# Softmax order in batch 0, and q loaded ahead of v with k projected alone in batch 1: Linformer attention and a maxout MoE layer in one kernel

## Chip, cores and metric

The kernel runs on one core of one Trainium2 chip. The metric is the device time of one execution in microseconds (us); times given for a kernel are medians over executions, and the profile is of one execution.

## The reference, cut to what matters

Eight batches, eight heads, sequence 1024, head dimension 64. Keys and values are first projected along the sequence to 64 rows, so the softmax runs over 64 columns.

```python
k_proj = np.einsum('ks,bhsd->bhkd', E, k)
v_proj = np.einsum('ks,bhsd->bhkd', F, v)
scores = (q @ k_proj.T) / sqrt(64)          # per batch and head
scores = scores - max(scores); attn = exp(scores); attn = attn / sum(attn)
x = (attn @ v_proj), as (8192 tokens, 512)
out = maximum(x @ w1, x @ w2) @ w_out       # w1, w2: 512x1024, w_out: 1024x512
```

All inputs and the output are float32; the kernel works in float16 with float32 sums.

## The kernel before, in words

**Engines.** TensorE does matmuls and transposes into PSUM. VectorE and ScalarE take results out of PSUM. GpSimd (POOL) issues the loads, which change float32 to float16 on their way; SyncE (SP) issues stores and DMA transposes. Each engine runs its instructions in the order in which the program gives them; the order is written out by hand.

**PSUM.** Four single banks (`mm_bank`, handed out in turn from the list `turn`, or by number) and two pairs of banks (`att_banks`, used alternately). A bank or pair is written again only after its last reader.

**A batch's attention.** Heads are worked in groups of four (g = 0, 1) and the tokens in halves (j = 0, 1), so there are four blocks (g, j). The steps, by the names used in the lists of the code: `kv` projects k and v (`step_kv` for a part of the heads in batch 0, `step_kv_sets` for all of them later; k goes to `kp_sb`, v to `vp_sb`), `kpt` transposes the projected k into `kpt`, `qt` transposes q into `qt_sb` on TensorE (batches 0 and 1). For a block: `tp` (`step_top`) computes scores and VectorE takes the row maxima (L340, two reductions); `tt` (`step_topt`) transposes the maxima and ScalarE copies them (L358); `sc` (`step_sc`) computes the scores less their maxima (L372) and ScalarE takes the exponential (L415, 1.02 us); `dn` (`step_dn`) sums the exponentials by a matmul with ones, and ScalarE takes the logarithm (L423); `in` (`step_inv`) takes exp(-log), the inverse (L427); `at` (`step_at`, `AT` with a PSUM pair) multiplies by the values (L387), and VectorE multiplies by the inverse into `xt_sb` (L442).

**The MoE layer.** max(a, b) = b + relu(a - b), so `wd` = w1 - w2 is made on VectorE (`step_wd`), `gt` = relu(x wd) is the up product (L522 in batch 0; `u0`, `u1` are the two halves of the tokens, eight column blocks each), and the output is gt w_out + x (w2 w_out), where w2 w_out is multiplied out once into `m_sb` (`step_w2t` transposes w2 on TensorE with a copy by ScalarE, L554 and L560; `m_steps`, L631). Later batches form up and down products by Strassen's scheme, with sums of blocks on VectorE (`sums_x`, `sums_g`, L703, and `step_t`, L594) and the partial products kept by ScalarE (L717) or added by VectorE (L865).

**Order around the change.** Batch 0's attention is a straight list of calls. After it comes the list `slots`: up products of batch 0, then the pieces of the down product of its first half, keys ("P", 0, p, i), into which batch 1's attention is put: after piece n = 1, 2, ... come the steps named in the n-th string of a list. A piece of unit 0 is six matmuls; p1, p2, ... end with a copy by ScalarE or an addition by VectorE. A step that returns a function leaves its last part (the reductions of `tp`, the copy of `tt`, the copies of v) to be issued after the next slot's own work.

**Loads.** The GpSimd queue is served in order: batch 0's k, q, v, then the weights, then k, v, q of batch 1 and k of batch 2 (`loads`). q of batch 1 comes in two halves by chunk. The tiles are four buffers (`kvq`); v and q of batch 2 are issued after batch 1's projection, because they take the buffers of batch 1's k and of another tile that is then free. q of batch 2 is transposed by DMA (L310).

Three of the calls in batch 0 that the text refers to:

```python
step_kv(t, 0, 4, "v")        # L981, values of heads 0 to 3
step_kv(t, 4, 8, "v", True)  # L1000, values of heads 4 to 7, into a PSUM pair
step_w2t(0, True)            # L1006
```

Of the kernel before, what the change touches and what calls it, by code (L numbers as in the profile page):

```python
# [9 lines left out]
FP16 = mybir.dt.float16  # L10
LN_EXP_SET = 6
ACTF = mybir.ActivationFunctionType
# [4 lines left out]
def kernel(  # L17
# [12 lines left out]
    nc = tc.nc  # L30
# [28 lines left out]
    def mm_bank(dtype=FP32, n=None):  # L59
        if n is None:  # L60
            n = turn.pop(0)
            turn.append(n)
        return ps.tile([128, 512 if dtype == FP32 else 1024], dtype, tag=f"mm{n}", name="mm_ps")

    def att_banks(dtype=FP32):
        return ps.tile(
            [128, 2, 512 if dtype == FP32 else 1024], dtype, tag="att", bufs=2, name="att_ps"
        )
# [116 lines left out]
        t["qt"] = qtp.tile([128, H, HALF], FP16, tag="qt", name="qt_sb")  # L185


    def step_kv(t, h0, h1, which, att=False):
        kv_ps = att_banks()[:, 0, :] if att else mm_bank()
        n = (h1 - h0) * D  # L190
        both = which == "v"
        i = "kv".index(which)
        for c in range(NC):
            for r in range(2) if both else (0,):
                nc.tensor.matmul(
                    out=kv_ps[r * KP : (r + 1) * KP, 0:n],
                    lhsT=eft[i][:, c, :],
                    rhs=t[which][:, h0:h1, c, :],
                    start=(c == 0), stop=(c == NC - 1),
                )  # L200
        if both:
            nc.vector.tensor_copy(
                out=t["vp"][:, h0:h1],
                in_=kv_ps[:, 0:n].rearrange("p (h d z) -> p h z d", d=D // 2, z=2),
            )
        else:
            t["kp"] = soft.tile([KP, 4, 2, D], FP16, tag="soft", name="kp_sb")
            for r, copy in enumerate((nc.vector.tensor_copy, nc.vector.tensor_copy if h0 else nc.scalar.copy)):
                copy(out=t["kp"][:, :, r, :], in_=kv_ps[0:KP, 0:n].rearrange("p (h d) -> p h d", d=D))
# [1 line left out]

    ORDER = (0, 2, 1, 3)

    def step_kv_sets(t, bank=None, copy=nc.scalar.copy):
        late = bank is None
        if late:
            bank = att_banks()[:, 0, :]
        t["sets"] = True
        kp = t["kp"] = proj.tile([128, H // 2 + 1, D], FP16, tag="kp", name="kp_sb")
        n = H // 2 * D  # L220
        for i, w in enumerate("kv"):
            for c in range(NC):
                for s in range(2):
                    nc.tensor.matmul(  # L224
                        out=bank[s * KP : (s + 1) * KP, i * n : (i + 1) * n],
                        lhsT=eft[i][:, c, :],
                        rhs=t[w][:, s * H // 2 : (s + 1) * H // 2, c, :],
                        start=(c == 0 and i == 0), stop=(c == NC - 1), skip_group_check=True,
                    )
        k_ps = bank[:, 0:n].rearrange("p (h d) -> p h d", d=D)  # L230
        copy(out=kp[:, 0 : H // 2, :], in_=k_ps)
        copy(out=kp[:, H // 2, :], in_=k_ps[:, 0, :])

        def finish_v():
            vp, m = t["vp"], H // 2
            nc.vector.tensor_copy(
                out=vp[:, 0:m], in_=bank[:, n : 2 * n].rearrange("p (h d z) -> p h z d", d=D // 2, z=2)
            )
            for a, b in (0, KP), (KP, 0):
                nc.vector.tensor_copy(out=vp[a : a + KP, m:H], in_=vp[b : b + KP, 0:m])  # L240

        if late:
            return finish_v
        finish_v()

    def step_kpt_sets(t):
        kpt_ps = att_banks(FP16)[:, 0, :]
        for i, a in enumerate(ORDER):
            nc.tensor.transpose(  # L249
                out=kpt_ps[:, i * 2 * KP : (i + 1) * 2 * KP],  # L250
                in_=t["kp"][:, a : a + 2, :].rearrange("p h d -> p (h d)"), identity=ident16,
            )
        def finish():
            src = kpt_ps[:, 0 : H * KP].rearrange("q (y x s k) -> q x y s k", y=2, x=2, s=2)
            dst = t["kpt"].rearrange("q (s x y) r k -> q r x y s k", s=2, x=2)
            lo, hi = slice(0, D), slice(D, 128)
            nc.scalar.copy(out=dst[lo, 0], in_=src[lo])
            nc.scalar.copy(out=dst[hi, 1, :, 1], in_=src[hi, :, 0])
            for x in range(2):
                nc.scalar.copy(out=dst[hi, 1, 1 - x, 0], in_=src[hi, x, 1])  # L260

        return finish

    def kpt_of(t, head, o):
        return t["kpt"][o * D : (o + 1) * D, head, o, :]
# [82 lines left out]
    def step_topt(t, g, j):  # L348
        x = t.pop(("top", g, j))
        ps_t = mm_bank(FP16) if t is tiles[0] else att_banks(FP16)[:, 0, :]  # L350
        for i in range(2):
            nc.tensor.transpose(  # L352
                out=ps_t[:, i * 128 : (i + 1) * 128], in_=x[:, i, :], identity=ident16
            )
        t["topt", g, j] = y = proj.tile([128, W], FP16, tag="topt", bufs=4, name="topt_sb")

        def finish():
            nc.scalar.copy(out=y, in_=ps_t[:, 0:W])  # L358

        return finish  # L360
# [47 lines left out]
        return t["xt"][:, 2 * g : 2 * g + 2, :, j * W : (j + 1) * W]  # L408


    def step_sc(t, g, j):
        sc_ps = att_banks()
        t["ps", g, j] = sc_ps
        score(t, g, j, [sc_ps[:, e, :] for e in range(2)])
        nc.scalar.activation(out=t["ex", g, j], in_=sc_ps, func=ACTF.Exp, scale=scale)  # L415

    def step_dn(t, g, j):
        dn_ps = t.pop(("ps", g, j))[:, :, 0:W]
# [6 lines left out]
    def step_inv(t, g, j):  # L425
        ld = t["ld", g, j]
        nc.scalar.activation(out=ld, in_=ld, func=ACTF.Exp, scale=-1.0)  # L427
# [109 lines left out]
    def step_wd(f0, r0=0, r1=NDC, n=256):  # L537
        nc.vector.tensor_tensor(
            out=wd_sb[:, r0:r1, f0 : f0 + n], in0=w1_sb[:, r0:r1, f0 : f0 + n],
            in1=w2_sb[:, r0:r1, f0 : f0 + n], op=ALU.subtract,  # L540
        )
# [433 lines left out]
    step_sc(t, 0, 1)  # L975
    step_dn(t, 0, 0)
    tops = [step_top(t, 1, j) for j in range(2)]
    tops.pop(0)()
    step_topt(t, 1, 0)()
    step_dn(t, 0, 1)  # L980
    step_kv(t, 0, 4, "v")  # L981
    tops.pop(0)()
    step_sc(t, 1, 0)
    for f0 in (0, 128):
        step_wd(f0, 0, 2, 128)
    step_topt(t, 1, 1)()
    step_inv(t, 0, 0)
    first_banks = turn[0:2], turn[2:4]
    step_at(t, 0, 0)
    step_sc(t, 1, 1)  # L990
    step_inv(t, 0, 1)
    step_dn(t, 1, 0)
    step_at(t, 0, 1)
    step_dn(t, 1, 1)
    step_inv(t, 1, 0)
    step_inv(t, 1, 1)
    u0, u1 = [*up_slots(t, 0)], [*up_slots(t, 1)]
    for x in u0[0:2]:
        x(r1=2)
    step_kv(t, 4, 8, "v", True)  # L1000
    for x in u1[0:2]:
        x(r1=2)
    step_wd(0, 2, 4)
    step_at(t, 1, 0, True)
    step_at(t, 1, 1, True)
    step_w2t(0, True)  # L1006


    load_all(tiles[1], 1, "k", k)
# [5 lines left out]
    def loads(b, *names):  # L1015
# [14 lines left out]
                load_all(tiles[b_], b_, n, {"k": k, "v": v, "q": q}[n])  # L1030

    slots = [
        (0, lambda: u0[0](r0=2)), (1, lambda: u0[1](r0=2)), (None, lambda: loads(1, "v", "q", "k")),
        (None, lambda: step_w2t(256, True)),
        (2, lambda: u1[0](r0=2)), (3, lambda: u1[1](r0=2)),
        (None, wd[1]), (4, u0[2]), (5, u0[3]),
        (None, wd[2]), (6, u1[2]), (7, u1[3]), (None, wt[2]), (None, wt[3]), (8, u0[4]), (9, u0[5]), (None, wd[3]),
        (10, u1[4]), (11, u1[5]), (12, u0[6]), (13, u0[7]),
# [45 lines left out]
    at_slot((0, 22), new_attn, t)  # L1084
    at_slot((0, 22), lambda: turn.__setitem__(slice(None), [2, 3]))
    for n, x in enumerate((
        "", "qt00 qt10", "kv", "qt01", "kpt qt11", "tp00", "tp10", "tt00", "tt10 tp01", "tp11", "tt01",
        "tt11", "sc00", "sc10", "dn00 in00", "dn10 in10", "at00", "AT10", "sc01",
    )):
        key = ("P", n // 15, (n - 1) // 2 % 7, (n - 1) % 2) if n else (0, 22)  # L1090
        for name in x.split():
            if name[0] == "k":
                if name == "kpt":
                    at_slot(key, step_kpt_sets, t)
                else:
                    at_slot(key, step_kv_sets, t, None, nc.vector.tensor_copy)
                    at_slot(key, loads, 2, "v", "q")
            else:
                g, j = int(name[2]), int(name[3])
                s_ = {"qt": step_qt, "sc": step_sc,  # L1100
                      "tp": step_top, "tt": step_topt, "dn": step_dn, "in": step_inv, "at": step_at, "AT": step_at}[name[:2]]
                args = (4 * g, 4, 2 * j, 2 * j + 2) if name[:2] == "qt" else (g, j)
                if name[:2] == "qt":
                    s_ = lambda *a: step_qt(*a, copy=nc.scalar.copy)
                at_slot(key, s_, t, *args, *([True] if name[:2] == "AT" else []))
        if n in (1, 4):
            at_slot(key, step_t, 1, (0, 1) if n == 1 else (2, 3))
        if 14 <= n < 18:
            at_slot(key, step_tw, n - 14)
        if 6 <= n < 10:  # L1110
            at_slot(key, sums_x, U[0, 1], ((2, 0, 1, 3)[n - 6],))


    t = tiles[2]
# [107 lines left out]
```

## Time and profile before

| | us |
|---|---|
| median of 3 runs (356.95 to 357.12) | 356.96 |
| the profiled execution | 357.18 |
| its span | 355.4 |
| TensorE busy | 342.1 (96%) |
| VectorE busy | 274.9 (77%) |
| ScalarE busy | 227.6 (64%) |
| batch 0's attention, TensorE | to about 32 |
| batch 1's attention, TensorE | about 51 to 75 |
| granted TensorE clock | 0.999 |

The page gives each engine's busy time, the chain of work that ended last, and the costliest groups of instructions with the idle time before them and what ended it. The timeline gives instructions in order of time, with the idle time of the engine before each and its releaser. A load's landing is its issue plus the time that the DMA view gives for it.

### The profile page before, as it was taken

To read this page: it belongs to the slowest core of one execution; us is meant where nothing else is said; L and a number is where in the kernel's file an instruction comes from. 1 tells how busy PE (TensorE), PEld (TensorE's weight loads), DVE (VectorE), ACT (ScalarE), POOL (GpSimd) and SP (SyncE) were. 2 spreads that over 40 slices of the span, in tenths; PEclk is the share of its full clock that TensorE was granted. 3 is DMA by queue.
4 is the path that set the end of the run, shared out by engine and by line. 5 is a ranking of instruction groups with operands and counts; after the bars stand their busy time and mean duration, and the time that the engine had idled before them with its cause. 6 is when DMAs were issued, how large, how long until landed. Compare 5 with 4: busy or idle time off the path is not lost.

```text
span 355.4 us, 11049 instructions
## 1 busy us (share of the span) xinstructions
PE 342.1 (96%) x4801; PEld 283.3 (80%) x4801; DVE 274.9 (77%) x511; ACT 227.6 (64%) x435; POOL 39.0 (11%) x58
## 2 busy tenths in 40 slices
PE   7878998999999999999999999999999999999996
PEld 3644587667888888888888888888888888888885
DVE  4765875877796969696978969696969869696873
ACT  2376755477776676767675867667674767676542
POOL 8375002020000110003000200003000000000000
PEclk9999999999999999999999999999999999999999
DMA  8999999999201999588993999499976511031223
GB/s 190 206 197 203 208 201 191 196 153 207 45 30 49 191 166 218 155 164 163 203 263 106 181 185 226 121 174 174 211 159 102 138 55 67 16 105 35 86 90 118
DMA packets 73713, 52.87 MB, mean 149 GB/s; under 512 B 26817, under 2 KB 73281, under 8 KB 73665
## 3 DMA queue, kind: packets, MB, share of 16 engines
q0 software_dynamic: 30688, 28.05, 50.0%
q1 hardware_dynamic: 42688, 23.93, 27.6%
q8 instruction: 37, 0.61, 0.7%
q10 hardware_dynamic: 288, 0.20, 0.2%
q14 instruction: 12, 0.09, 0.1%
HBM read 57.15 MB, written 16.78 MB: 208 GB/s over the span
## 4 chain that ended last, share of the span: by engine, by line
PE 75%; DVE 0%; ACT 0%; issue 0%; DVEq 0%
PE mm_ps L835 38%; PE mm_ps L743 24%; PE mm_ps L372 4%; PE att_ps L331 3%; PE mm_ps L224 3%; PE att_ps L387 3%; PE att_ps L352 1%; PE att_ps L249 0%; DVE o_sb L933 0%; PE mm_ps L927 0%; ACT p_sb L717 0%; ACT kpt L260 0%; DVEq L933 0%
## 5 line engine op out<-in xcount | busy, mean ns | idle before, releaser
L717 ACT COPY p_sb<-mm_ps 128x512 f32<-128x512 f32 x179 | 101.3, 592 | 57.7 <-PE mm_ps L743 32.4
L835 PEld LDWEIGHTS <-big 128*128 128x128 f16 x768 | 72.3, 98 | 10.6 <-issue 3.2
L835 PE MATMUL mm_ps<-T_sb,big 128*128 128x256 f16 x576 | 77.2, 273 | 0.0
L758 DVE TENSOR_TENSOR gt_sb<-mm_ps,p_sb 128x512 f16<-128x512 f32 x56 | 38.4, 686 | 42.7 <-PE mm_ps L743 41.3
L743 PE MATMUL mm_ps<-big,big 128*128 128x256 f16 x336 | 50.4, 273 | 0.7 <-ACT p_sb L717 0.7
L743 PEld LDWEIGHTS <-big 128*128 128x128 f16 x448 | 43.8, 98 | 6.0 <-issue 0.9
L835 PE MATMUL mm_ps<-wo_sb,gt_sb 128*128 128x256 f16 x256 | 43.0, 273 | 0.0
L468 ACT ACTIVATE ex_sb<-mm_ps 128x512 f16<-128x512 f32 x50 | 27.1, 594 | 20.1 <-PE att_ps L387 11.4
L835 PEld LDWEIGHTS <-gt_sb 128*128 128x128 f16 x376 | 34.3, 98 | 7.0 <-issue 3.6
L340 DVE TENSOR_REDUCE top<-att_ps 128x8 f16<-128x512 f32 x56 | 36.1, 689 | 3.6 <-PE att_ps L331 3.6
L743 PEld LDWEIGHTS <-wd_sb 128*128 128x128 f16 x336 | 32.9, 98 | 3.8
L743 PE MATMUL mm_ps<-xt_sb,wd_sb 128*128 128x256 f16 x224 | 32.8, 273 | 0.0
L497 DVE TENSOR_TENSOR xt_sb<-att_ps,ld_sb 128x1024 f16<-128x1024 f32 x26 | 31.6, 1214 | 0.0
L865 DVE TENSOR_TENSOR o_sb<-mm_ps,p_sb 128x512 f32<-128x512 f32 x32 | 21.8, 681 | 4.4 <-PE mm_ps L835 2.4
L835 PE MATMUL mm_ps<-m_sb,xt_sb 128*128 128x256 f16 x128 | 24.5, 273 | 0.0
L290 POOL COPY junk<-qt_sb 1x1 f16<-1x1 f16 x6 | 1.8, 298 | 202.1 <-DMA qt_sb<-q_sb 202.1
L761 DVE TENSOR_SCALAR gt_sb<-gt_sb 128x512 f16<-128x512 f16 (+1 forms) x60 | 21.8, 363 | 2.1
L703 DVE TENSOR_TENSOR big<-gt_sb 128x1024 f16<-128x1024 f16 x32 | 21.8, 681 | 0.0
L835 PE MATMUL mm_ps<-wo_sb,big 128*128 128x256 f16 x128 | 21.5, 273 | 0.0
L835 PE MATMUL mm_ps<-T_sb,gt_sb 128*128 128x256 f16 x120 | 20.3, 273 | 0.0
L835 PEld LDWEIGHTS <-xt_sb 128*128 128x128 f16 x188 | 18.2, 98 | 2.4 <-issue 0.2
L804 ACT ACTIVATE gt_sb<-mm_ps 128x512 f16<-128x512 f32 x28 | 17.0, 606 | 4.6 <-PE mm_ps L743 4.6
(138 smaller groups left out, 554.0 us busy)
## 6 DMA issues: line engine op xcount, KB each, us to landing
out_dram<-o_sb SPq DMA_DIRECT2D x62, 256.0 KB, 2.6
k_sb<-in_k_dram POOLq DMA_DIRECT2D x7, 1024.0 KB, 9.3
v_sb<-in_v_dram POOLq DMA_DIRECT2D x7, 1024.0 KB, 14.1
q_sb<-in_q_dram POOLq DMA_DIRECT2D x5, 1024.0 KB, 21.4
q_sb<-in_q_dram POOLq DMA_DIRECT2D x6, 512.0 KB, 11.8
big<-in_moe_w_dram POOLq DMA_DIRECT2D x12, 128.0 KB, 6.3
v_sb<-in_v_dram POOLq DMA_DIRECT2D x4, 256.0 KB, 13.8
wo_sb<-in_moe_w_out_dram POOLq DMA_DIRECT2D x1, 1024.0 KB, 10.4
```

The costliest lines, as they stand in the source:

```text
L340: nc.vector.tensor_reduce(out=top[k][:, i, :].rearrange("p (o h) -> p h o", o=2)[:, 0:4, :], in_=banks[i].rearrange("p (h o k) -> p h o k" ...
L372: nc.tensor.matmul(out=banks[e][pos : pos + Z, h * W : (h + 1) * W], lhsT=pick[rows, 2 * h + e, :] if shift else kpt_of(t, head, o)[:, s * ...
L468: nc.scalar.activation(out=t["ex", g, j][:, e, :], in_=banks[e], func=ACTF.Exp, scale=scale)
L497: nc.vector.tensor_tensor(out=x_out(t, g, j).rearrange("q z o n -> q o z n"), in0=at_ps.rearrange("q o (z n) -> q o z n", z=2), in1=ld[:, ...
L703: nc.vector.tensor_tensor(out=S(i), in0=S(0) if x is None else x, in1=y(), op=op)
L717: copy(out=x, in_=bank)
L743: nc.tensor.matmul(out=bank[:, m * W : (m + 1) * W], lhsT=w_[:, n_, (2 * d + m) * 128 : (2 * d + m + 1) * 128], rhs=a[:, n_, :], start=(n ...
L758: nc.vector.tensor_tensor(out=c_blk(j, c), in0=two(x), in1=two(y), op=ALU.add)
L761: nc.vector.tensor_scalar_max(ap, ap, 0.0)
L804: nc.scalar.activation(out=out, in_=in_, func=ACTF.Relu)
L835: nc.tensor.matmul(out=bank[i][:, 0:CH] if two_banks else bank[:, i * CH : (i + 1) * CH], lhsT=a(c)[:, i * 128 : (i + 1) * 128], rhs=w_(c) ...
L865: nc.vector.tensor_tensor(out=o_sb, in0=two(x), in1=two(y), op=ALU.add)
```

## The change

In batch 0 the four reductions of heads 4 to 7 are issued in a row, ahead of the copy of the first projected values; the second projection of v (heads 4 to 7) comes between the scores of block (1, 1) and the sums of block (1, 0) and uses a single bank, the one that `turn` names next, instead of a pair; the last exponential is issued after the logarithm of block (1, 0); values, inverses and the first half of the up products are interleaved anew; `step_w2t(0)` moves behind the second half of `u0`, `step_w2t(256)` behind that of `u1`.

In batch 1 q is loaded ahead of v; `step_kv_sets` can project k or v alone: k at n = 1 (`kk`), its transposes and all four copies at n = 3 (`kpt`), v at n = 8 (`kv`); the q tiles of j = 1 are copied by VectorE instead of ScalarE; the steps from `qt` on are one slot later up to `sc10` and `dn`, and `at00` keeps its slot; the sums of x move from n = 6 to 9 to n = 2 to 5; v of batch 2 is issued after `kk`, q of batch 2 at n = 5.

```diff
-    def step_kv(t, h0, h1, which, att=False):
-        kv_ps = att_banks()[:, 0, :] if att else mm_bank()
+    def step_kv(t, h0, h1, which, bank=None):
+        kv_ps = mm_bank(n=bank)
...
-    def step_kv_sets(t, bank=None, copy=nc.scalar.copy):
+    def step_kv_sets(t, bank=None, copy=nc.scalar.copy, which="kv"):
...
         for i, w in enumerate("kv"):
+            if w not in which:
+                continue
...
+        if "k" in which:
+            kp = t["kp"] = proj.tile([128, H // 2 + 1, D], FP16, tag="kp", name="kp_sb")
+            k_ps = bank[:, 0:n].rearrange("p (h d) -> p h d", d=D)
+            copy(out=kp[:, 0 : H // 2, :], in_=k_ps)
+            copy(out=kp[:, H // 2, :], in_=k_ps[:, 0, :])
+            if which == "k":
+                return
...
-    def step_sc(t, g, j):
+    def step_sc(t, g, j, later=False):
...
-        nc.scalar.activation(out=t["ex", g, j], in_=sc_ps, func=ACTF.Exp, scale=scale)
+
+        def finish():
+            nc.scalar.activation(out=t["ex", g, j], in_=sc_ps, func=ACTF.Exp, scale=scale)
+
+        if later:
+            return finish
+        finish()
...
     step_dn(t, 0, 0)
     tops = [step_top(t, 1, j) for j in range(2)]
-    tops.pop(0)()
+    for finish in tops:
+        finish()
     step_topt(t, 1, 0)()
     step_dn(t, 0, 1)
     step_kv(t, 0, 4, "v")
-    tops.pop(0)()
+    step_inv(t, 0, 0)
+    step_topt(t, 1, 1)()
     step_sc(t, 1, 0)
+    step_at(t, 0, 0)
     for f0 in (0, 128):
         step_wd(f0, 0, 2, 128)
-    step_topt(t, 1, 1)()
-    step_inv(t, 0, 0)
-    first_banks = turn[0:2], turn[2:4]
-    step_at(t, 0, 0)
-    step_sc(t, 1, 1)
+    finish = step_sc(t, 1, 1, True)
+    step_kv(t, 4, 8, "v", turn[0])
     step_inv(t, 0, 1)
     step_dn(t, 1, 0)
+    finish()
     step_at(t, 0, 1)
-    step_dn(t, 1, 1)
-    step_inv(t, 1, 0)
-    step_inv(t, 1, 1)
+    first_banks = turn[0:2], turn[2:4]
     u0, u1 = [*up_slots(t, 0)], [*up_slots(t, 1)]
     for x in u0[0:2]:
         x(r1=2)
-    step_kv(t, 4, 8, "v", True)
+    step_wd(0, 2, 4)
+    step_inv(t, 1, 0)
+    step_at(t, 1, 0, True)
+    step_dn(t, 1, 1)
+    step_inv(t, 1, 1)
     for x in u1[0:2]:
         x(r1=2)
-    step_wd(0, 2, 4)
-    step_at(t, 1, 0, True)
     step_at(t, 1, 1, True)
-    step_w2t(0, True)
...
-        (0, lambda: u0[0](r0=2)), (1, lambda: u0[1](r0=2)), (None, lambda: loads(1, "v", "q", "k")),
+        (0, lambda: u0[0](r0=2)), (1, lambda: u0[1](r0=2)), (None, lambda: loads(1, "q", "v", "k")),
+        (None, lambda: step_w2t(0, True)),
+        (2, lambda: u1[0](r0=2)), (3, lambda: u1[1](r0=2)),
         (None, lambda: step_w2t(256, True)),
-        (2, lambda: u1[0](r0=2)), (3, lambda: u1[1](r0=2)),
...
-        "", "qt00 qt10", "kv", "qt01", "kpt qt11", "tp00", "tp10", "tt00", "tt10 tp01", "tp11", "tt01",
-        "tt11", "sc00", "sc10", "dn00 in00", "dn10 in10", "at00", "AT10", "sc01",
+        "", "kk", "qt00 qt10", "kpt", "qt01", "qt11 tp00", "tp10", "tt00", "kv tt10", "tp01", "tp11", "tt01",
+        "tt11", "sc00", "sc10", "dn00 in00", "dn10 in10 at00", "AT10", "sc01",
...
-                    at_slot(key, step_kv_sets, t, None, nc.vector.tensor_copy)
-                    at_slot(key, loads, 2, "v", "q")
+            if name == "kk":
+                at_slot(key, step_kv_sets, t, None, nc.vector.tensor_copy, "k")
+                at_slot(key, loads, 2, "v")
+            elif name == "kv":
+                at_slot(key, step_kv_sets, t, None, nc.vector.tensor_copy, "v")
+            elif name == "kpt":
+                at_slot(key, step_kpt_sets, t, 0)
...
-                if name[:2] == "qt":
+                if name[:2] == "qt" and j == 0:
                     s_ = lambda *a: step_qt(*a, copy=nc.scalar.copy)
...
-        if 6 <= n < 10:
-            at_slot(key, sums_x, U[0, 1], ((2, 0, 1, 3)[n - 6],))
+        if n == 5:
+            at_slot(key, loads, 2, "q")
+        if 2 <= n < 6:
+            at_slot(key, sums_x, U[0, 1], ((2, 0, 1, 3)[n - 2],))
```

`step_kpt_sets` gets an argument `parts`: with 2 its last two copies are left for a further slot, with 0 all four are issued at once.

More of the change, by code (lines that the diff above doesn't have):

```diff
@@ L218, in step_kv_sets @@
         t["sets"] = True
-        kp = t["kp"] = proj.tile([128, H // 2 + 1, D], FP16, tag="kp", name="kp_sb")
         n = H // 2 * D
         for i, w in enumerate("kv"):
+            if w not in which:
+                continue
             for c in range(NC):
@@ L227, in step_kv_sets @@
                         rhs=t[w][:, s * H // 2 : (s + 1) * H // 2, c, :],
-                        start=(c == 0 and i == 0), stop=(c == NC - 1), skip_group_check=True,
+                        start=(c == 0 and w == which[0]), stop=(c == NC - 1), skip_group_check=True,
                     )
-        k_ps = bank[:, 0:n].rearrange("p (h d) -> p h d", d=D)
-        copy(out=kp[:, 0 : H // 2, :], in_=k_ps)
-        copy(out=kp[:, H // 2, :], in_=k_ps[:, 0, :])
+        if "k" in which:
[5 more added lines that the diff above has]
+                return
         def finish_v():
@@ L244, in step_kv_sets, with step_kpt_sets @@
         finish_v()
-    def step_kpt_sets(t):
+    def step_kpt_sets(t, parts=2):
         kpt_ps = att_banks(FP16)[:, 0, :]
@@ L258, in finish, with rest @@
             nc.scalar.copy(out=dst[hi, 1, :, 1], in_=src[hi, :, 0])
-            for x in range(2):
-                nc.scalar.copy(out=dst[hi, 1, 1 - x, 0], in_=src[hi, x, 1])
-        return finish
+            def rest():
+                for x in range(2):
+                    nc.scalar.copy(out=dst[hi, 1, 1 - x, 0], in_=src[hi, x, 1])
+            if parts == 2:
+                return rest
+            rest()
+        if parts == 0:
+            finish()
+        else:
+            return finish
     def kpt_of(t, head, o):
@@ L414, in step_sc @@
         score(t, g, j, [sc_ps[:, e, :] for e in range(2)])
-        nc.scalar.activation(out=t["ex", g, j], in_=sc_ps, func=ACTF.Exp, scale=scale)
+        def finish():
+            nc.scalar.activation(out=t["ex", g, j], in_=sc_ps, func=ACTF.Exp, scale=scale)
+        if later:
+            return finish
+        finish()
     def step_dn(t, g, j):
@@ L981 @@
     step_kv(t, 0, 4, "v")
-    tops.pop(0)()
+    step_inv(t, 0, 0)
+    step_topt(t, 1, 1)()
     step_sc(t, 1, 0)
+    step_at(t, 0, 0)
     for f0 in (0, 128):
         step_wd(f0, 0, 2, 128)
-    step_topt(t, 1, 1)()
-    step_inv(t, 0, 0)
-    first_banks = turn[0:2], turn[2:4]
-    step_at(t, 0, 0)
-    step_sc(t, 1, 1)
+    finish = step_sc(t, 1, 1, True)
+    step_kv(t, 4, 8, "v", turn[0])
     step_inv(t, 0, 1)
     step_dn(t, 1, 0)
+    finish()
     step_at(t, 0, 1)
-    step_dn(t, 1, 1)
-    step_inv(t, 1, 0)
-    step_inv(t, 1, 1)
+    first_banks = turn[0:2], turn[2:4]
     u0, u1 = [*up_slots(t, 0)], [*up_slots(t, 1)]
@@ L1091 @@
         for name in x.split():
[L1092 to L1095, printed above, removed]
-                    at_slot(key, step_kv_sets, t, None, nc.vector.tensor_copy)
-                    at_slot(key, loads, 2, "v", "q")
+            if name == "kk":
[5 more added lines that the diff above has]
+                at_slot(key, step_kpt_sets, t, 0)
             else:
                 g, j = int(name[2]), int(name[3])
-                s_ = {"qt": step_qt, "sc": step_sc,
-                      "tp": step_top, "tt": step_topt, "dn": step_dn, "in": step_inv, "at": step_at, "AT": step_at}[name[:2]]
+                s_ = {"qt": step_qt, "tp": step_top, "tt": step_topt, "sc": step_sc, "dn": step_dn,
+                      "in": step_inv, "at": step_at, "AT": step_at}[name[:2]]
                 args = (4 * g, 4, 2 * j, 2 * j + 2) if name[:2] == "qt" else (g, j)
-                if name[:2] == "qt":
+                if name[:2] == "qt" and j == 0:
                     s_ = lambda *a: step_qt(*a, copy=nc.scalar.copy)
```

## The prediction

> **What bounds the kernel now.** I read the page first (busy shares, chain), then TensorE's waits by stretch, then the timeline of the stretches in which it waits, then the landings of the loads.
>
> The page: columns are engine, busy us, share of the span, instructions; below it the chain that ended last.
>
> ```profile
> PE 342.1 (96%) x4801; PEld 283.3 (80%) x4801; DVE 274.9 (77%) x511; ACT 227.6 (64%) x435; POOL 39.0 (11%) x58
> ...
> PE 75%; DVE 0%; ACT 0%; issue 0%; DVEq 0%
> ```
>
> TensorE bounds it, and the chain is TensorE back to 84 us. Busy time by stretch (window, length, PE busy and count, and so on; PEclk is the granted clock):
>
> ```profile
> 20.00:33.00 13.00, 9.89 (x219) 5.93 (x219) 8.43 (x16) 8.27 (x15) 11.27 (x15) 1.00 1.37 199
> 33.00:50.00 17.00, 17.00 (x119) 10.69 (x117) 12.20 (x23) 11.92 (x20) 0.00 (x0) 1.00 1.29 205
> 50.00:68.00 18.00, 15.51 (x186) 13.07 (x183) 11.26 (x25) 9.16 (x17) 2.38 (x3) 1.00 1.23 197
> ...
> 84.00:355.00 271.00, 267.88 (x3778) 232.55 (x3777) 217.95 (x397) 180.09 (x354) 12.12 (x17) 1.00 0.66 135
> ```
>
> The edits lie in 20 to 31 us (batch 0) and 50 to 75 us (batch 1). TensorE idles 3.1 us in the first row and 2.5 us in the third; in the second it never waits, so time won before 33 us is carried through to 50. Its waits from 84 us on are one line:
>
> ```profile
> PE mm_ps L743 <- ACT p_sb L717: 0.7, 1, 0.7
> ```
>
> So what TensorE gains before 84 us reaches the end, unless a load is late: those alone keep their own clock. The waits to be removed, in the timeline (start, length, engine, line, [idle before <- releaser]); first batch 0, then batch 1:
>
> ```profile
> 22.37 0.23 PE L352 MATMUL mm_ps<-ident,top 128*128 128x128 f16 x1 [0.57 <-DVE top L340]
> 22.97 0.23 PE L352 MATMUL mm_ps<-ident,top 128*128 128x128 f16 x1 [0.37 <-DVE top L340]
> 25.21 0.30 PE L387 MATMUL att_ps<-ex_sb,ones 64*32 64x256 f16 x8 [0.82 <-ACT ex_sb L415]
> 30.44 0.61 PE L554 MATMUL att_ps<-ident,big 128*128 128x128 f16 x8 [1.36 <-DVE xt_sb L442]
> ```
> ```profile
> 59.65 0.61 PE L331 MATMUL att_ps<-kpt,qt_sb 128*128 128x128 f16 x8 [1.63 <-ACT kpt L260]
> ...
> 63.18 0.28 PE L352 MATMUL att_ps<-ident,top 128*128 128x128 f16 x2 [0.40 <-DVE top L340]
> 63.73 0.61 PE L331 MATMUL att_ps<-kpt,qt_sb 128*128 128x128 f16 x8 [0.27 <-ACT topt_sb L358]
> ```
>
> The first two wait for maxima that VectorE took only after the values' copy; the third for an exponential that stands behind an inverse; the fourth for a PSUM pair that four VectorE products must clear. In batch 1, ScalarE copies two q tiles (56.08 and 57.40, 1.01 us each) ahead of kpt (58.31 to 59.59).
>
> **Part A, batch 0.** No arithmetic is added: same 16 transfers, same instructions, new order, and one PSUM buffer changed. I walk the queues; a TensorE step is priced by its distance to the next start in the timeline: values projection 1.00 (20.18 to 21.18), score 0.45 (17.33 to 17.77), sums or values of a group 0.23, four up matmuls 0.96, eight transposes 0.44. A hand-over between engines is 0.05 to 0.08 (exponential's end 25.16, sums 25.21).
>
> To 21.18 nothing changes for TensorE; VectorE's four maxima run 18.43 to 20.95 (2.5 us in a row), still ahead of the projection that its copy needs (21.29 to 21.71, as before). TensorE: topt(1,1) 21.18 without a wait; score(1,0) 21.30; values(0,0) 21.78, after the copy; score(1,1) 22.00; second values projection 22.44 to 23.44 (heads 6 and 7 of v landed at 21.3: 6.93 + 14.3); sums(1,0) to 23.67. ScalarE: inverse(0,0) to 21.47, topt copy to 21.92, exponential(1,0) 22.0 to 23.0, inverse(0,1) to 23.6, log(1,0) 23.8 to 24.4, and behind it the last exponential 24.3 to 25.32: the added order costs the exponential 0.2 against 24.14, covered by the next two TensorE steps. VectorE: products(0,0) 22.27 to 23.56, two wd pieces to 23.96, values copy to 24.30. Here is the new wait: values(0,1) uses the bank of that copy, so TensorE idles about 0.7 until 24.36. Then up u0 24.59, values(1,0) 25.55, sums(1,1) 25.78 (exponential done 25.32), u1 26.24 (0.2 for products(0,1), done 26.14), values(1,1) 27.20, second half of u0 27.77 (0.3 for products(1,0), done 27.68), w2t(0) 28.73, u1 29.16 (its products are done at 28.98, under w2t), w2t(256) 30.05, next up product 30.50. Before, that product started at 32.19 + 4 x 0.216 = 33.05. **A gains 2.55.** Moving w2t behind u0 costs nothing: ScalarE's copy (1.0) has 0.9 of up matmuls and then banks that it does not hold. Bounds: were each of the four waits left 0.25 longer (one wd piece, 0.28) A gains 1.5; with the three waits before 30.44 and that one gone, 3.1.
>
> **The loads.** v1 (28.52 + 18.7 = 47.2), then the halves of q1 (29.77 + 20.1 = 49.9; 30.63 + 21.9 = 52.5) land now; batch 1 reads q1 at 51.26. With A alone TensorE would be there at 48.7 and wait 1.2. The queue moves 1 MB in 5.1 us (k1 lands 42.1, v1 47.2), so in the new order q1 lands at 44.7 and 47.3, v1 at 52.4, k2 at 57.7 as before. POOL has the same issues, none of which waits (all buffers are free by 23.5). v1 is now read at about 58.7: 6 us of slack. v2 and q2 stay behind k2 in the queue and land near 63 and 68, as now; batch 2 needs them at 73 and 80.
>
> **Part B, batch 1.** Everything starts 2.55 earlier: product n=1 at 47.87. TensorE: k alone 48.60 (0.93 for 16 of the 32 matmuls that took 1.87), q transposes 50.25, kpt transposes 51.80, q 52.68 and 53.78, scores for the maxima (tp00) 54.22. ScalarE: two q copies 50.95 to 52.88, kpt copies 52.8 to 54.07, so the 1.63 wait ends, with 0.1 to spare. What is late next is VectorE, which gets the other two q copies and has the sums of x at n = 2 to 5 in place of 6 to 9: o_sb 52.9, q copy 53.5, T pair 54.1, sum 54.8, q copy 55.1, sum 55.7, then maxima tp00 56.05 to 57.35 and tp10 to 58.6, each spaced 0.35 or 0.61 as in the timeline. TensorE reaches the transposes of tp00 at 56.4 and ends them at 57.5 (1.0 of wait), the v projection's PSUM pair is held by tp10's maxima to 58.6 (0.5 of wait), and its copies hide under a product (59.75 to 60.2). tt11 waits 0.3 for the last maxima, and the product behind it (n=13) starts at 63.78. Before, the same work was done at 68.0 (67.32 + six matmuls, 0.65). 68.0 - 63.78 = 4.2, so **B gains 1.7** of 2.5 us of waits. Bounds: 0 (the VectorE run above takes back as much as kpt gave) to 2.5 (no new wait). Behind n=13 the exponentials have 0.2 to 0.6 of slack as now; I count nothing there.
>
> One price of B is open to a rule: the two q copies that go to VectorE. The groups show this copy, 128x1024 from PSUM, at 0.686 on VectorE (batch 0) and 1.014 on ScalarE (batch 1); I use 0.61 of spacing. The Trainium skill, page Perfetto Trace Analysis, section Optimizing Scalar/DVE Operations, speaks against the move: an access to PSUM costs VectorE about 125 ns and ScalarE about 51. By that alone, as an estimate, the run of VectorE would be 0.15 longer and the sum 0.15 smaller; the row says that the copy itself is 0.33 shorter, and the row decides.
>
> **Sum.** A 2.55 + B 1.7 = 4.25. My hand-overs are the shortest in the trace; 0.15 occurs too (30.29 to 30.44). Eight waits are left in the walk, 0.03 more for each is 0.25. Gain 4.0. The profiled execution took 357.18 (span 355.4, 1.8 around it), the median is 356.96, 0.22 less; 356.96 - 4.0 = 353.0.
>
> **Rivals.**
> VectorE gives B back (0.17): its run from 52.9 has no gap, so anything late in it moves all maxima; then only A is left, 356.96 - 2.5 = 354.4. For it: 5.7 us of work in a row. Against: it idled 2.13 and 2.67 in this stretch before.
> The waits go wholly (0.13): A 2.8, B 2.5, 351.7, if the values copy overtakes nothing and VectorE keeps up.
> Slower (0.07): v1 now stands behind q1, and its projection stands in TensorE's queue ahead of tt10 and all that follows. If v1 lands after 58.7, each us later is a us of the end; slower than before by 0.7 needs a landing at 58.7 + 4.0 + 0.7 = 63.4, 11 us later than the queue's pace says. Against: 5.1 us per MB held from 32 to 57 us. A landing at 66 would give 359.5.
> Nothing gained (0.04): the same mechanism, less late, or a wait that I do not see, 357.0.
> My forecast (0.59): 352.3 to 353.9.
>
> Range: the low bounds, A 1.5 and B 0, give 355.4; the high ones, 3.1 + 2.5 = 5.6, give 351.4. A measurement of this kernel tells about 0.2%, 0.7 us. Faster by more than that: 0.59 + 0.17 + 0.13 = 0.89; within 0.04; slower 0.07.
>
> **What would show it.** Right: no idle at the first topt pair (1,1) and the fourth wait gone; TensorE idle near 0.7 ahead of values(0,1), released by VectorE's vp copy; next up product near 30.5; q1 landing near 45 and 47; no wait for kpt; waits of some 1.5 in all for maxima around 56 to 59; the wait at 84.15 at about 80, still 0.7; TensorE busy still 342. Wrong: a DMA as releaser of TensorE after 20 us, TensorE waits over 2 us in batch 1, or a larger wait at the 84 us place.

## The result, and the profile after

| | before | after |
|---|---|---|
| median, us (20 runs each) | 357.06 | 355.98 |
| profiled execution's span, us | 355.4 | 354.0 |
| TensorE busy, us | 342.1 | 341.8 |

The ratio is 0.9967, 95% interval [0.9957, 0.9977]: 1.1 us faster where 4.0 were forecast; the median lies above the forecast's range of 351.4 to 355.4. Busy time of the changed kernel by stretch (window, length, then PE, PEld, DVE, ACT, POOL busy with counts, granted clock, DMA share, GB/s):

```profile
20.00:33.00 13.00, 12.27 (x223) 6.94 (x224) 8.63 (x18) 10.73 (x18) 10.99 (x15) 1.00 1.37 199
33.00:50.00 17.00, 17.00 (x137) 11.65 (x135) 13.33 (x27) 10.03 (x16) 0.26 (x1) 1.00 1.31 204
50.00:68.00 18.00, 16.90 (x272) 13.54 (x271) 14.24 (x29) 9.79 (x19) 2.10 (x3) 1.00 1.23 200
...
84.00:354.00 270.00, 263.59 (x3685) 228.52 (x3682) 214.67 (x391) 177.57 (x347) 11.97 (x17) 1.00 0.66 135
```

TensorE idles 0.7 us in the first row (3.1 before) and 1.1 us in the third (2.5 before), so the edited stretches did gain. But in the last row 6.4 of 270 us are not busy, where it was 3.1 of 271. TensorE's waits from 84 us on are again one line (who <- releaser: us in total, times, longest), another one than before:

```profile
PE att_ps L345 <- ACT kpt L267: 3.1, 5, 0.6
```

Once in each of batches 3 to 7, at 118.00, 158.02, 198.04, 238.06 and 278.08 us, the first scores for the maxima wait for kpt. ScalarE's timeline of the changed kernel ahead of the first of them, and TensorE's row:

```profile
115.45 0.59 ACT L737 COPY p_sb<-mm_ps 128x512 f32<-128x512 f32 x1
115.94 0.58 ACT L262 COPY kpt<-att_ps 64x512 f16<-64x512 f16 x1
116.53 0.37 ACT L263 COPY kpt<-att_ps 64x256 f16<-64x256 f16 x1
116.92 0.58 ACT L737 COPY p_sb<-mm_ps 128x512 f32<-128x512 f32 x1
117.53 0.42 ACT L267 COPY kpt<-att_ps 64x128 f16<-64x128 f16 x2
```
```profile
118.00 0.61 PE L345 MATMUL att_ps<-kpt,qt_sb 128*128 128x128 f16 x8 [0.61 <-ACT kpt L267]
```

The same place in the kernel before, ScalarE and TensorE:

```profile
121.00 0.58 ACT L257 COPY kpt<-att_ps 64x512 f16<-64x512 f16 x1
121.58 0.37 ACT L258 COPY kpt<-att_ps 64x256 f16<-64x256 f16 x1
121.86 0.43 ACT L260 COPY kpt<-att_ps 64x128 f16<-64x128 f16 x2
122.31 1.07 ACT L717 COPY p_sb<-mm_ps 128x512 f32<-128x512 f32 x2
```
```profile
122.33 0.61 PE L331 MATMUL att_ps<-kpt,qt_sb 128*128 128x128 f16 x8
```

Before, the four kpt copies ran in a row and TensorE started 0.04 after their end. Now a p_sb copy stands between the second and the third. This comes from the argument `parts` of `step_kpt_sets`. Its default is 2, so the last two copies are left over and issued behind the next slot's own work, here a p_sb copy. Batch 1 passes 0; batches 2 to 7, which the rest of the change does not touch, call the helper without the argument and get the default.

The idle time in a row counts from the modelled end of the matmuls before it, and the rows overlap a little when nothing waits (before: 121.85 + 0.60 = 122.45, but the next row starts at 122.33). Start to start, the step to these scores takes 1.21 (116.79 to 118.00) in place of 0.48 (121.85 to 122.33), so a wait shown as 0.61 costs 0.73.

The account in one place, with the start of each batch's k projection as the mark: batch 3's starts at 109.75 in place of 114.81, 5.06 earlier. From there the distance between the k projections of two batches is 40.02 in place of 39.28 to 39.29, four times over, and 2.94 is lost; the last stretch, from batch 7's k projection to the end, takes 84.18 in place of 83.45 and loses 0.73. 5.06 - 2.94 - 0.73 = 1.39, the spans' 355.4 - 354.0.

### The profile page after: what moved, and what is told of

Read it like the earlier page. It is cut to its first block, busy times and chain, and to the rows that moved or that the text cites. A ratio compares the mean times of both kernels' runs of the same rounds, so it can differ in the third digit from the quotient of the medians.

```text
span 354.0 us, 11051 instructions
## 1 busy us (share of the span) xinstructions
PE 341.8 (97%) x4801; PEld 282.8 (80%) x4801; DVE 276.0 (78%) x513; ACT 226.8 (64%) x433; POOL 38.9 (11%) x58
## 3 DMA queue, kind: packets, MB, share of 16 engines
q0 software_dynamic: 30688, 28.05, 50.3%
## 4 chain that ended last, share of the span: by engine, by line
PE 69%; ACT 4%; DVE 4%; issue 0%; DVEq 0%
PE mm_ps L855 34%; PE mm_ps L763 21%; PE mm_ps L386 4%; PE att_ps L345 3%; PE mm_ps L225 3%; ACT p_sb L737 2%; PE att_ps L401 2%; DVE xt_sb L517 2%; ACT ex_sb L488 1%; DVE gt_sb L778 1%; PE att_ps L366 1%; ACT kpt L267 1%; DVE gt_sb L781 0%; DVE big L723 0%; DVE o_sb L953 0%
## 5 line engine op out<-in xcount | busy, mean ns | idle before, releaser
L345 PEld LDWEIGHTS <-qt_sb 128*128 128x128 f16 x256 | 16.6, 98 | 5.4 <-issue 4.2
L855 PE MATMUL mm_ps<-T_sb,gt_sb 128*128 128x256 f16 x120 | 20.3, 273 | 0.0
```

The source lines that it names most:

```text
L345: nc.tensor.matmul(out=banks[i][:, h * 128 : (h + 1) * 128], lhsT=t["qt"][:, 4 * g + h, j * W + i * 128 : j * W + (i + 1) * 128], rhs=t["k ...
L855: nc.tensor.matmul(out=bank[i][:, 0:CH] if two_banks else bank[:, i * CH : (i + 1) * CH], lhsT=a(c)[:, i * 128 : (i + 1) * 128], rhs=w_(c) ...
```

## The experiments

All are timed against the kernel before, whose median was 357.12 to 357.32 in these comparisons.

**Is it the split of kpt's copies?** First, the changed kernel with the split taken out from batch 3 on (with `parts` 1 all four copies are issued together, in the slot in which they were before the change).

```diff
-        at_slot(("U", n, 0, 2), step_kpt_sets, t)
+        at_slot(("U", n, 0, 2), step_kpt_sets, t, 1)
```

> The changed kernel with one thing undone: from batch 3 on, all four ScalarE copies of kpt are issued at once, as before. Theory (the split of these copies, which the prediction passed over, puts a p_sb copy between the second and the third in each of batches 3 to 7): the wait of 0.6 for kpt at 118, 158, 198, 238 and 278 us goes, the distance between two batches' k projections goes from 40.02 back to 39.28, five times 0.735 = 3.7 are won, 355.98 - 3.7 = 352.3. Rival (ScalarE is late there because TensorE, now ahead, or the other use of the PSUM pairs, pushes it): the waits stay at another copy, 355.5 to 356.

Measured: 352.24, ratio 0.9854 [0.9836, 0.9872]; the distance between k projections is 39.28 to 39.29, and TensorE has no wait left after 84 us. ScalarE and TensorE of this kernel at the place:

```profile
116.43 0.37 ACT L263 COPY kpt<-att_ps 64x256 f16<-64x256 f16 x1
116.70 0.43 ACT L267 COPY kpt<-att_ps 64x128 f16<-64x128 f16 x2
117.15 1.07 ACT L737 COPY p_sb<-mm_ps 128x512 f32<-128x512 f32 x2
```
```profile
117.18 0.61 PE L345 MATMUL att_ps<-kpt,qt_sb 128*128 128x128 f16 x8
```

The third copy starts at 116.70 with TensorE 5 us ahead of before, so ScalarE was not pushed late by that; the p_sb copy in between was all. Second, the split alone, in the kernel before:

```diff
...
+            def rest():
+                for x in range(2):
+                    nc.scalar.copy(out=dst[hi, 1, 1 - x, 0], in_=src[hi, x, 1])
+            if parts == 2:
+                return rest
+            rest()
...
-        at_slot(("U", n, 0, 2), step_kpt_sets, t)
+        at_slot(("U", n, 0, 2), step_kpt_sets, t, 2)
```

> The kernel before with the split of kpt's copies alone, from batch 3 on. Theory of the split: five waits of 0.6, the distance 39.28 to 40.02, 357.06 + 3.7 = 360.7. Rival (the split costs only together with the earlier TensorE): 357.0 to 357.5.

Measured: 360.98, ratio 1.0114 [1.0086, 1.0141]; five waits of 0.62 and a distance of 40.02. The split costs 3.7 with the rest of the change (355.98 - 352.24) and without it (360.98 - 357.32).

**Does it help where batch 2 uses it?** On top of the first experiment:

```diff
-    at_slot(("U", 1, 0, 1), step_kpt_sets, t)
+    at_slot(("U", 1, 0, 1), step_kpt_sets, t, 1)
```

> As e1_kpt_whole_later (352.24), and batch 2 copies kpt whole too. Theory (in batch 2 a p_sb copy is what TensorE waits for, behind the kpt copies, so the split helps there): the wait near 79 us goes from 0.39 back to the 0.72 of before, 352.6. Rival (that wait shrank for another reason): 0.39 stays, 352.2.

Measured: 352.94, ratio 0.9894 [0.9868, 0.992]. The distance from batch 2's k projection to batch 3's goes from 36.61 to 36.92, which is that of the kernel before: the split is worth 0.3 in batch 2. There TensorE waits first for a p_sb copy, in batches 3 to 7 for kpt. ScalarE and TensorE of the changed kernel in batch 2:

```profile
78.43 0.58 ACT L737 COPY p_sb<-mm_ps 128x512 f32<-128x512 f32 x1
79.04 0.42 ACT L267 COPY kpt<-att_ps 64x128 f16<-64x128 f16 x2
```
```profile
79.07 0.60 PE L763 MATMUL mm_ps<-big,big 128*128 128x256 f16 x4 [0.39 <-ACT p_sb L737]
```

With kpt whole that wait shows as 0.59 and not as the expected 0.72, and the median is 0.7 above the first experiment's. In the two profiled executions 0.3 of this is the distance above, and 0.35 was there ahead of batch 1's k projection (48.65 against 48.30), where the kernels do not differ.

**The two parts alone.** Batch 0's new order, loads as before:

```diff
...
+    step_inv(t, 0, 0)
+    step_topt(t, 1, 1)()
     step_sc(t, 1, 0)
+    step_at(t, 0, 0)
...
+    finish = step_sc(t, 1, 1, True)
+    step_kv(t, 4, 8, "v", turn[0])
...
         (0, lambda: u0[0](r0=2)), (1, lambda: u0[1](r0=2)), (None, lambda: loads(1, "v", "q", "k")),
...
```

> The kernel before with the change of batch 0 alone; batch 1 with v loaded ahead of q as before. By the prediction's walk and the changed kernel's trace (next up product at 30.26 in place of 33.05) TensorE is 2.6 to 2.8 ahead at 50 us and finds q of batch 1 not landed: first half due at 49.9, asked for at 48.6, a wait of 1.2 to 1.3 with a DMA as releaser; net gain 1.4, 355.6. Rival (the queue of loads moves ahead as well, or the gain is taken back by another wait in batch 0): no wait for q and 354.4, or no gain and 357.

Measured: 356.41, ratio 0.997 [0.9957, 0.9984]. TensorE's timeline at batch 1's first q transposes:

```profile
50.28 1.07 PE L298 MATMUL mm_ps<-ident,q_sb 128*128 128x128 f16 x16 [1.58 <-DMA q_sb<-in_q_dram]
```

The first half of q landed at 50.3 (issued at 29.96, plus 20.3), 0.4 later than in the trace before, so the wait is 1.58 and not 1.2 to 1.3; batch 3's k projection is 0.96 ahead, and 0.36 of it is lost in the last distance (39.64 in place of 39.28), at a wait of 0.24 for VectorE near 262 us. So the gain is 0.9 where 1.4 was expected. On top of that, q ahead of v, but k and v still projected together:

```diff
-        (0, lambda: u0[0](r0=2)), (1, lambda: u0[1](r0=2)), (None, lambda: loads(1, "v", "q", "k")),
+        (0, lambda: u0[0](r0=2)), (1, lambda: u0[1](r0=2)), (None, lambda: loads(1, "q", "v", "k")),
```

> The kernel before with the change of batch 0 and q loaded ahead of v, but k and v of batch 1 still projected together at n = 2. q lands at 45 and 47.5, v at 52.5 to 53. Theory (the queue of loads moves 1 MB in 5.1 us whatever is asked first, so the order only decides who waits): no wait for q at 48.6, and TensorE asks for v at about 51.2 and waits 1.3 to 1.8 with a DMA as releaser; the time stays at that of batch 0 alone, 356.4. Rival (q was the whole matter, and projecting k apart is not needed for the loads): no wait for a DMA, 354.7.

Measured: 356.93, ratio 0.9993 [0.9982, 1.0004]. TensorE's timeline at the projection:

```profile
51.57 1.06 PE L224 MATMUL att_ps<-k_sb,eft 128*64 128x256 f16 x16
53.21 1.06 PE L224 MATMUL att_ps<-v_sb,eft 128*64 128x256 f16 x16 [0.57 <-DMA v_sb<-in_v_dram]
```

The time is not told apart from the kernel before. The DMA wait passes from q to v. It is shorter than expected because this execution began late (TensorE waited 1.69 us for its first k, and values(0,1) started at 25.66 in place of 24.44 in the run above), yet the v projection starts at 53.21, 0.4 later than in the run above (52.83): v landed at 53.1 (31.02 + 22.1), and the load sets that time, whatever is won ahead of it. In the changed kernel, which projects k alone, v is asked for at 58.4 and TensorE waits for neither load. So projecting k alone is what lets q go first.

Batch 1's edits alone, kpt whole from batch 3 on:

```diff
-        (0, lambda: u0[0](r0=2)), (1, lambda: u0[1](r0=2)), (None, lambda: loads(1, "v", "q", "k")),
+        (0, lambda: u0[0](r0=2)), (1, lambda: u0[1](r0=2)), (None, lambda: loads(1, "q", "v", "k")),
...
-        "", "qt00 qt10", "kv", "qt01", "kpt qt11", "tp00", "tp10", "tt00", "tt10 tp01", "tp11", "tt01",
+        "", "kk", "qt00 qt10", "kpt", "qt01", "qt11 tp00", "tp10", "tt00", "kv tt10", "tp01", "tp11", "tt01",
```

> The kernel before with the change of batch 1 alone (q ahead of v, k projected alone, copies and sums moved), kpt's copies whole from batch 3 on. The prediction gave 1.7 to this part: 355.3. The changed kernel's trace gives 5.06 in all at batch 3's k projection, less 2.79 for batch 0: 2.3, and 354.8. Rival (VectorE gives it back): 356.5 or more.

Measured: 355.46, ratio 0.9953 [0.9937, 0.9969], 0.7 above what was expected; batch 3's k projection is 2.12 ahead where 2.3 was expected, and 0.36 is lost again in the last distance. 355.46 - 352.24 = 3.2 is what batch 0's order is worth once q is there, 0.36 of it from that late wait; without q it was worth 0.9. The two parts do not add up: 0.9 and 1.9 alone, 5.1 together.

**What holds the rest back?** TensorE's timeline of the changed kernel, the rows with its largest waits in the edited stretches of batch 0 and batch 1; the prediction had each of them:

```profile
24.19 0.41 PE L401 MATMUL mm_ps<-ex_sb,vp_sb 64*32 64x256 f16 x16 [0.56 <-DVE vp_sb L202]
```
```profile
57.22 0.29 PE L366 MATMUL att_ps<-ident,top 128*128 128x128 f16 x2 [0.85 <-DVE top L354]
...
58.42 1.06 PE L225 MATMUL att_ps<-v_sb,eft 128*64 128x256 f16 x16 [0.25 <-DVE top L354]
```

The last two stand behind an unbroken run of VectorE that ends with the maxima. Two sums of x taken out of that run, on top of the first experiment:

```diff
-        if 2 <= n < 6:
-            at_slot(key, sums_x, U[0, 1], ((2, 0, 1, 3)[n - 2],))
+        if 2 <= n < 4:
+            at_slot(key, sums_x, U[0, 1], ((2, 0), (1, 3))[n - 2])
```

> As e1_kpt_whole_later, with the four sums of x at n = 2 and 3, two each, in place of one each at n = 2 to 5. Theory (the waits of 0.84 and 0.25 for maxima at 57.1 and 58.3 come from an unbroken run of VectorE from about 53 us on, and VectorE is idle at 51 to 53): two sums, 0.7, leave the run, the waits fall to 0.4 or less together, 351.5. Rival (the maxima wait for something else, or the sums then delay the q copies): waits unchanged or moved to the q copies, 352.2 or more.

Measured: 351.74, ratio 0.9842 [0.9827, 0.9857]. The first wait falls from 0.84 to 0.17, the second stays at 0.25; the distance from batch 1's k projection to batch 2's falls from 24.75 to 24.09. The q copies back on ScalarE, again on top of the first experiment:

```diff
-                if name[:2] == "qt" and j == 0:
+                if name[:2] == "qt":
```

> As e1_kpt_whole_later (352.24), with all q copies of batch 1 on ScalarE. Theory of VectorE's run: 1.2 (two copies at 0.6 of spacing) leave it, so the waits of 0.84 and 0.25 for maxima go; ScalarE has the kpt copies done at 53.8 and is idle until 55.3, so it takes the two copies of 1.01 with a p_sb copy late by some 0.5, for which nobody waits: 351.2. Rival (the move to VectorE was needed, ScalarE's copies hold up a p_sb copy or the score of block (0, 1)): 352.2 or more.

Measured: 351.5, ratio 0.9837 [0.9811, 0.9863]. That distance falls to 23.69, the first wait is gone, the second is 0.20, and TensorE is busy 11.80 of the 12.00 us from 50 to 62, in place of 10.91 in the first experiment. But 0.36 is lost near 257 us as in the partial runs, which is about what the time lies above the expected 351.2. TensorE's timeline in this kernel:

```profile
56.26 0.28 PE L366 MATMUL att_ps<-ident,top 128*128 128x128 f16 x2
56.38 0.82 PE L855 MATMUL mm_ps<-T_sb,big 128*128 128x256 f16 x6
57.39 1.06 PE L225 MATMUL att_ps<-v_sb,eft 128*64 128x256 f16 x16 [0.20 <-DVE top L354]
```

Both together:

```diff
-                if name[:2] == "qt" and j == 0:
+                if name[:2] == "qt":
...
-        if 2 <= n < 6:
-            at_slot(key, sums_x, U[0, 1], ((2, 0, 1, 3)[n - 2],))
+        if 2 <= n < 4:
+            at_slot(key, sums_x, U[0, 1], ((2, 0), (1, 3))[n - 2])
```

> As e7_sums_at_2_and_3 (351.74), with all q copies of batch 1 on ScalarE. Theory: the waits for maxima that e7 left, 0.17 and 0.25, go, and the two edits do not add up: 351.2 to 351.4. Rival: VectorE still bounds, and the two edits add up to 350.6; or ScalarE does, 351.7 or more.

Measured: 351.55, ratio 0.9836 [0.981, 0.9861]: no more than either alone, as expected, though not within the expected 351.2 to 351.4; the distance is 23.56, both waits are gone, and the 0.36 is lost near 257 us here too. Of the kernels tried, this one and the two before it are the fastest, 5.4 to 5.6 us below the kernel before, and not told apart by their intervals. The first experiment's interval overlaps theirs too, so what they gain over it rests on the traces.

In batch 0, the wd pieces behind the second values' copy:

```diff
-    for f0 in (0, 128):
-        step_wd(f0, 0, 2, 128)
     finish = step_sc(t, 1, 1, True)
     step_kv(t, 4, 8, "v", turn[0])
+    for f0 in (0, 128):
+        step_wd(f0, 0, 2, 128)
```

> As e1_kpt_whole_later, with the two wd pieces of batch 0 issued on VectorE behind the copy of the second values instead of ahead of it. Theory (the wait of 0.55 at 24.1 is for that copy, which stands behind 0.48 of wd pieces in VectorE's queue): the copy starts at the projection's end, 23.4, the wait falls to 0.2, and the wd pieces end before the up products ask for them; 0.3 won, 351.9. Rival (the up products then wait for wd): 352.2 or more.

Measured: 352.24, ratio 0.9862 [0.9845, 0.9878], nothing won. The copy did start earlier (23.44) and the wait fell from 0.55 to 0.29, but values(1,0) now has a break of 0.2 after its first two matmuls, and sums(1,1) starts at 25.83 against 25.68. The up products did not wait for wd, so the rival's reason is not it either; what holds values(1,0) there was not tried and stays open.

## Why the prediction was wrong, by its own steps

**The step that failed** is "The edits lie in 20 to 31 us (batch 0) and 50 to 75 us (batch 1)", and with it "So what TensorE gains before 84 us reaches the end, unless a load is late". The diff also changes `step_kpt_sets`, a helper that batches 2 to 7 call with its default. The sum has no term for it. In batches 3 to 7 it measures 5 x 0.735 = 3.7 (taken out, 355.98 to 352.24; put in alone, 357.32 to 360.98). The trace of before had the price ready: at 121.00 to 122.33 kpt's copies end 0.04 ahead of TensorE, so a p_sb copy of 0.59 put between them must show as a wait of about that. None of the rivals was it: the slower one rested on a late load, and no load was late. (By its own sum, a landing of v at 66 would have given 360.3 and not 359.5.) None of the signs that the prediction named for being wrong occurred either; they all looked at the edited stretches, at the loads and at the one wait at 84 us.

**Part A** was forecast at 2.55, with the next up product at 30.50: it started at 30.26, 2.79 earlier than before. The first k projection started 0.28 sooner in this execution (7.67 for 7.95), so A is 2.5. Its waits came at the places named: values(0,1) at 24.19 for 24.36, released by VectorE's vp copy, and the 0.2 and 0.3 that followed, taken start to start as the walk does, were 0.1 (the up product at 26.09) and 0.3 (at 27.61). One step of the walk does not fit its own prices: the second half of u1 (29.16 to 30.05) has 0.89 where four up matmuls are 0.96; both such steps took 0.86.

**The loads** were right: q landed at 44.8 and 47.5 (forecast 44.7 and 47.3), v at 52.5 (52.4), and no DMA releases TensorE after 20 us. Left in the old order, q costs 1.58 where 1.2 was forecast.

**Part B** was forecast at 1.7. The walk's last product (n=13) starts at 63.45, 4.5 ahead of the 68.0 before; less 2.79, B is 1.7 there. Behind it, where the prediction counted nothing, 0.2 more came by batch 2's k projection and 0.3 from the split in batch 2, which makes the 5.06 at batch 3's. The waits for maxima came at the places named: 1.0 and 0.5 in the walk, start to start 1.0 and 0.4 (the rows show 0.85 and 0.25 of idle time). The last wait, for tt11, did not occur. The run of VectorE is shown as the cause of the first: take two sums out of it, and that wait falls to 0.17; take two copies out, and it goes.

**The sum**, 353.0, has no term for the split at all, so it stands against the kernel whose kpt copies are whole in every later batch: 352.94, 4.2 below the kernel before in that comparison, where 4.0 was forecast. With the split in batch 2 alone, which gains, it is 352.24 and 5.1. So the walks of A and B were right in mechanism and nearly in size; that the times agree to 0.1 us is luck, since the interval of that ratio, 0.9868 to 0.992, is 1.9 us wide.

**The rule on PSUM copies.** The Trainium skill, page Perfetto Trace Analysis, section Optimizing Scalar/DVE Operations, spoke against giving the q copies to VectorE, as I read its costs of an access to PSUM alone. The copies took 0.68 to 0.69 on VectorE in batch 1, too, against 1.01 to 1.03 on ScalarE: the row was right on the copy. The move still cost 0.7 (352.24 against 351.5 with the copies on ScalarE). In the first experiment's trace ScalarE idles 1.49 and 2.30 us in that stretch, at 53.7 to 55.2 and 55.8 to 58.1, while VectorE works without a gap from 52.7 to 58.2. The same section says that breaking up instructions can let work be done sooner where ScalarE is not full but makes others wait. In this case the same copies, left whole or issued as two parts with a p_sb copy between them, gained 0.3 by the split in batch 2 and lost 0.7 by it in each of five later batches: it depends on what the next engine asks for first.

## What to carry to other kernels

Before a trace is divided into "touched" and "untouched" stretches, go through the diff for helpers and default arguments, and list every call of each: a helper's price is multiplied by its calls. In a queue served in order, a split is a move: read which instruction slips in between, and who waits for the last piece. Two edits can need each other (here an engine that comes earlier and a load that lands earlier); price them alone and together.

## What was not expected of the hardware

The first load of k was issued at 1.24 to 1.25 us in all twelve profiled executions, but it landed 5.7 to 7.8 us later, and the first k projection started between 7.28 and 9.15 us. A time in one trace set against the same place in another's carries that much. Five kernels (the three with one part alone and both with all q copies on ScalarE) lose 0.36 once, at a wait of 0.25 for VectorE at 257 to 262 us; the others do not, and what decides it stays open.
